# Pooled attention with a gated feed-forward layer on one core: issue order written by hand, images on one queue, first queries and results transposed on TensorE, weights issued after the images, five tiles of lead

## Chip, cores and metric

The kernel runs on one core of one Trainium2 chip. The metric is device time in microseconds (us) of one execution; the kernel before has a median of 1116.38 us over three runs (1113.78 to 1118.0). TensorE (PE), VectorE (DVE), ScalarE (ACT), GpSimd (POOL) and SyncE (SP) each execute their own instruction list in order; SP, ACT and POOL also start DMAs.

## What is computed

```python
# q: 4 x 12288 x 128, kv: 4 x 384 x 32 x 128, all float32
kv_pool = kv.reshape(B, H//4, 4, W//4, 4, C).mean(axis=(2, 4))   # 4x4 means: 768 keys per image
k = v = kv_pool.reshape(B, 768, C) @ w_sr
a = softmax(q @ k.T / sqrt(C));   x = a @ v                      # 4 x 12288 x 128
out = (maximum(x @ w_gate, 0) * (x @ w_val)) @ w_out             # 128 -> 1536 -> 128
```

## The kernel before

The 4 x 12288 queries are cut into 96 tiles of 512 (24 per image b). The 768 pooled keys of an image are six chunks (`jc`) of 128; the 1536 hidden columns are twelve blocks (`fb`) of 128. For a tile k the stages are:

- `scores(k, jc)`: one 128x512 matmul (line 153) and the exponential on ACT (line 154) into `aT`.
- `values(k, jc, half)`: small matmuls (line 165) that add up over jc; after the last, DVE casts the sums to `x16` (line 172) and takes reciprocals of the row sums (line 173). A DMA transpose on SP's queue (line 177) then turns `x16` into `xT`, which the feed-forward stage reads. The softmax division is applied once, squared, at the very end (`inv2`), since the output is quadratic in x.
- `value_proj`, `gate_proj` and `out_proj(k, fb)`: matmuls of lines 185, 196 and 210. ACT copies the value block to `val` (line 189), DVE forms `hT = max(gate, 0) * val` (line 199), and after twelve blocks DVE scales the result into `o_sb` (line 217), which SP stores (line 220).

One pass of the main loop ("loop k", k from 3 to 98) has twelve steps. At each step it issues a piece of `out_proj(k-4)`, `value_proj(k-3)`, `scores(k)` or `values(k-1)` in turn, and `gate_proj(k-3)`. So the feed-forward stage runs `LAG = 3` tiles behind the scores. Ahead of the loop a prelude computes the keys of image 0 chunk by chunk: four DMAs of 256 KB bring a chunk as four lines (`kv_load`, line 103), DVE adds the lines (`pool_lines`, lines 112 and 114), PE transposes and adds the columns (line 128), ACT copies (line 133), PE projects with `w_sr` (lines 135 and 136, float32), ACT scales into `kv16` (line 140), and then come the scores of tiles 0 to 3, and the values of tiles 0 and 1 one chunk behind. The images 1 to 3 are pooled by POOL inside the loop, and `project` stands at step 7 of six loops of each image.

Queries come in groups of four tiles (2048 rows): `q_load` casts float32 to float16 on POOL's software queue (line 75), `q_turn` transposes the group with a DMA transpose on SP's queue (line 85). The feed-forward weights are three casting DMAs on POOL's queue (lines 256 to 258).

The program is written in this sequence, but the framework's scheduler reorders the instructions of each engine by its own estimates, subject to data dependencies. It moves the weights' DMAs to the start, puts half of image 0's loads on ACT's queue, and brings the loads of image 1 forward as buffers (three `kv_in` slots) come free. Eight semaphore lanes (`DMAHW0` to `DMAHW7`) serve the DMAs of SP and ACT: a DMA waits until the one issued eight before it has landed. All PSUM tiles share eight banks.

Of the kernel before, what the change touches and what calls it, by code (L numbers as in the profile page):

```python
# [16 lines left out]
def kernel(  # L17
# [18 lines left out]


    nc = tc.nc

# [13 lines left out]
    NG = NT // GRP  # L53
    LAG = 3
    qk_scale = 1.0 / math.sqrt(C)
# [11 lines left out]

    q16s, qTs = {}, {}

# [10 lines left out]
    def q_turn(g):  # L80
# [5 lines left out]
        qTs[g] = qT  # L86

    def qT_of(k):
        s0 = (k % GRP) * NS
        return qTs[k // GRP][:, s0 : s0 + NS, :].rearrange("c s p -> c (s p)")  # L90
# [6 lines left out]
    def kv_load(b, jc, engines):  # L97
        parts = work.tile([128, r, r, C], FP32, tag="kv_in", bufs=3)
        rows = kv[b, jc * HC : (jc + 1) * HC].rearrange(
            "(hp dh) (wp dw) c -> dh hp wp (dw c)", dh=r, dw=r  # L100
        )
        for dh in range(r):
            engines[dh % len(engines)].dma_start(  # L103
                parts[:, dh].rearrange("p dw c -> p (dw c)"), rows[dh]
            )
        kv_in[b, jc] = parts

    def pool_lines(eng, b, jc):
        parts = kv_in.pop((b, jc))
        s2 = work.tile([128, 2, r, C], FP32, tag="kv_s2")  # L110
        for i in range(2):
            eng.tensor_tensor(s2[:, i], parts[:, 2 * i], parts[:, 2 * i + 1], op=ALU.add)  # L112
        s1 = work.tile([128, r, C], FP32, tag="kv_s1")
        eng.tensor_tensor(s1, s2[:, 0], s2[:, 1], op=ALU.add)
        return s1
# [7 lines left out]

    def project(b, jc, pooled, copy_a, copy_b):
        tp = bank([128, 128])
# [6 lines left out]
        kvT = work.tile([128, 128], FP32, tag="kvT")  # L132
        copy_a(kvT, tp)  # L133
        pr = bank([128, 2, 128])
        nc.tensor.matmul(pr[:, 0, :], w_sr_f32, kvT, start=True, stop=True)  # L135
        nc.tensor.matmul(pr[:, 1, :], kvT, w_sr_f32, start=True, stop=True)  # L136
        copy_b(kv16[:, b, jc, 0 : 2 * C], pr.rearrange("p i c -> p (i c)"))

# [16 lines left out]

    def values(k, jc, half):
        if jc == 0:
# [12 lines left out]
        if jc == NJC - 1:  # L170
            own = slice(2 * half, 2 * half + 2)
            nc.vector.tensor_copy(x16s[k][:, own, :], x_ps[:, :, 0:C])  # L172
            nc.vector.reciprocal(rinvs[k][:, own], x_ps[:, :, C])  # L173
            if half == 1:
                x16 = x16s.pop(k)
                xT = work.tile([128, NS, 128], FP16, tag="xT", bufs=6, name="xT")
                nc.sync.dma_start_transpose(xT, x16.rearrange("p s c -> p (s c)"))
                xTs[k] = xT.rearrange("c s p -> c (s p)")
                rinv = rinvs.pop(k)
                inv2s[k] = work.tile([128, NS, 1], FP32, tag="inv2", bufs=6, name="inv2")  # L180
                nc.vector.tensor_tensor(inv2s[k][:, :, 0], rinv, rinv, op=ALU.mult)

# [22 lines left out]
    def out_proj(k, fb):  # L205
# [8 lines left out]
        if fb == NFB - 1:  # L214
            hTs.pop(k)
            o_sb = work.tile([128, NS, 128], FP32, tag="o_sb", bufs=3)
            nc.vector.tensor_tensor(  # L217
                o_sb, o_banks.pop(k), inv2s.pop(k).to_broadcast([128, NS, 128]), op=ALU.mult
            )
            nc.sync.dma_start(  # L220
# [3 lines left out]
            )  # L224


    w_sr_f32 = const.tile([128, C], FP32)
    nc.sync.dma_start(w_sr_f32, w_sr)
    q_load(0)
    hw = [nc.sync, nc.scalar]  # L230
    kv_load(0, 0, hw)
    kv_load(0, 1, hw)
    ident = const.tile([128, 128], FP32)
    make_identity(nc, ident)
    nc.gpsimd.memset(kv16[:, :, :, 2 * C : 2 * C + 4], 1.0)
    q_turn(0)
    q_load(1)

# [3 lines left out]

    LEAD = GRP
    for jc in range(NJC):
        if jc + 2 < NJC:
            kv_load(0, jc + 2, hw)
        s1 = pool_lines(nc.vector, 0, jc)
        project(0, jc, s1, nc.scalar.copy, act_scaled)
        for k in range(LEAD):
            scores(k, jc)  # L250
# [4 lines left out]
        if jc == 2:  # L255
            nc.gpsimd.dma_start(wv16, moe_w_val)
            nc.gpsimd.dma_start(wg16, moe_w_gate)
            nc.gpsimd.dma_start(wo16, moe_w_out.rearrange("(fb f) c -> f fb c", f=128))
    for k in range(2):
        for half in range(2):  # L260
            values(k, NJC - 1, half)
    q_turn(1)
    q_load(2)


    last = NT + LAG - 1
    kv_s3 = {}
    for k in range(LAG, last + 1):
        g, ph = divmod(k, GRP)
        if ph == 0 and k > LAG:  # L270
            q_turn(g + 1)
            q_load(g + 2)
        b = k // NST + 1
        at = k % NST - (NST - NJC - 6)
        for step in range(NFB):
# [5 lines left out]
            if step % 2 == 0:  # L281
                if LEAD <= k < NT:
                    scores(k, step // 2)
            elif 2 <= k - 1 < NT:
                half, i = divmod(step // 2, NJC // 2)
# [4 lines left out]
            if b < B:  # L290
# [40 lines left out]
```

## Time and profile before

| | before |
|---|---|
| median of 3 runs | 1116.38 us (1113.78 to 1118.0) |
| profiled execution, own time | 1116.32 us |
| its span, first to last instruction | 1114.4 us |
| PE busy | 1041.0 us (93%) |
| DVE busy | 918.9 us (82%) |
| ACT busy | 904.8 us (81%) |
| POOL busy | 104.3 us (9%) |
| mean granted TensorE clock | 0.989 of full |

A row of a timeline reads: start in us, length in us, engine and line, operation, written tile <- read tiles, shape, count merged into the row (x4), and in brackets the idle time of that engine just before, with what ended it. "SPq" and "ACTq" rows are the DMA instructions of those engines. In a windows row the columns are the stretch, its length, busy time and number of instructions of PE, PE's weight loads, DVE, ACT and POOL, the granted clock, the DMA engines' busy share and GB/s. A DMA queue's row gives packets, MB that were written, and the time of its packets as a share of 16 engines; q1 is SP's queue, q10 ACT's, q0 POOL's software queue.

### The profile page before, as it was taken

The page shows a single profiled execution, that of the slowest core. Times are in us where ns is not written, and L with a number is a line of the kernel's source. Part 1 is how long each engine was busy: PE and PEld are TensorE (multiplying, and loading weights), DVE is VectorE, ACT ScalarE, POOL GpSimd, SP SyncE. Part 2 cuts the span into 40 slices and gives each one's busy share as a digit, 9 for nine tenths or more (in the row PEclk, how much of TensorE's full clock was granted, in tenths as well). Part 3 has the DMA queues.
Part 4 walks back from the last instruction along what each step waited for, and adds up shares of the span by engine and source line. Part 5 has one row for each costly group of instructions (what it writes and reads, how often), then busy time and mean ns, then how long its engine had stood idle before and what let it go on. Part 6 is the DMA issues. An engine that isn't in the chain of part 4 may idle for free.

```text
span 1114.4 us, 26042 instructions
## 1 busy us (share of the span) xinstructions
PE 1041.0 (93%) x9930; PEld 688.4 (62%) x9930; DVE 918.9 (82%) x1782; ACT 904.8 (81%) x1741; POOL 104.3 (9%) x124
## 2 busy tenths in 40 slices
PE   0538999999999999999999999999999999999998
PEld 0315666666666666666666666666666666666665
DVE  1328788888888888888888888888798898888888
ACT  0527888878888888878888888888788888888886
POOL 1183000044200000033100000000000000000000
PEclk9969999999999999999999999999999999999999
DMA  9999324256543133132231331341332331211111
GB/s 236 240 226 242 61 49 81 63 124 141 121 81 67 44 77 72 44 68 62 49 82 38 74 81 34 78 76 35 67 72 54 67 63 41 51 44 36 38 44 44
DMA packets 135357, 91.01 MB, mean 82 GB/s; under 512 B 107200, under 2 KB 107328, under 8 KB 135232
## 3 DMA queue, kind: packets, MB, share of 16 engines
q1 hardware_dynamic: 128208, 72.44, 28.1%
q0 software_dynamic: 5296, 13.76, 7.1%
q10 hardware_dynamic: 1728, 3.15, 0.9%
q8 instruction: 77, 1.26, 0.5%
q14 instruction: 48, 0.39, 0.1%
HBM read 52.76 MB, written 25.17 MB: 70 GB/s over the span
## 4 chain that ended last, share of the span: by engine, by line
PE 87%; DMA 6%; SPq 2%; ACT 2%; DVE 2%; issue 0%; POOL 0%; POOLq 0%; DVEq 0%
PE bank_ps L185 22%; PE bank_ps L196 22%; PE bank_ps L210 21%; PE bank_ps L165 11%; PE bank_ps L153 10%; DMA parts<-in_kv_dram 2%; DMA xT<-x 2%; SPq L85 2%; ACT val L189 2%; DMA qT<-q 2%; DVE hT L199 1%; PE bank_ps L135 1%; ACT aT L154 0%; SPq L103 0%; PE bank_ps L136 0%
## 5 line engine op out<-in xcount | busy, mean ns | idle before, releaser
L199 DVE SCALAR_TENSOR_TENSOR hT<-bank_ps,val 128x512 f16<-128x512 f32 x1152 | 772.3, 687 | 132.4 <-ACT val L189 93.1
L189 ACT CAST val<-bank_ps 128x512 f16<-128x512 f32 x1152 | 676.7, 592 | 162.3 <-PE bank_ps L185 160.8
L210 PEld LDWEIGHTS <-hT 128*128 128x128 f16 x4608 | 349.3, 97 | 200.8 <-issue 6.7
L185 PE MATMUL bank_ps<-xT,wv 128*128 128x512 f16 x1152 | 437.6, 380 | 25.7 <-DMA xT<-x 25.7
L210 PE MATMUL bank_ps<-wo,hT 128*128 128x128 f16 x4608 | 440.4, 219 | 0.9 <-DVE hT L199 0.8
L196 PE MATMUL bank_ps<-xT,wg 128*128 128x512 f16 x1152 | 436.4, 379 | 0.0
L154 ACT ACTIVATE aT<-bank_ps 128x512 f16<-128x512 f32 x576 | 346.8, 606 | 3.1 <-PE bank_ps L153 3.1
L165 PE MATMUL bank_ps<-kv,aT 128*128 128x129 f16 x2304 | 224.3, 220 | 0.1
L153 PE MATMUL bank_ps<-qT,kv 128*128 128x512 f16 x576 | 216.3, 381 | 2.9 <-ACT kv L140 2.9
L165 PEld LDWEIGHTS <-aT 128*128 128x128 f16 x2304 | 177.1, 98 | 66.9 <-issue 1.1
L196 PEld LDWEIGHTS <-wg 128*128 128x128 f16 x1152 | 111.6, 97 | 86.7 <-issue 18.8
L185 PEld LDWEIGHTS <-wv 128*128 128x128 f16 x1152 | 112.9, 98 | 13.0 <-DMA xT<-x 7.7
L172 DVE CAST x<-bank_ps 128x256 f16<-128x256 f32 x192 | 79.7, 415 | 9.8 <-PE bank_ps L165 9.8
L75 POOL DMA_DIRECT2D q<-in_q_dram x24 | 13.2, 549 | 675.0 <-DMA qT<-q 674.2
L217 DVE TENSOR_TENSOR o_sb<-bank_ps,inv 128x512 f32<-128x512 f32 x96 | 65.4, 681 | 0.5 <-PE bank_ps L210 0.5
L153 PEld LDWEIGHTS <-kv 128*128 128x128 f16 x576 | 56.0, 98 | 8.2 <-ACT kv L140 4.1
L112 POOL TENSOR_TENSOR s<-parts 128x512 f32<-128x512 f32 x36 | 45.1, 1267 | 10.5 <-DMA parts<-in_kv_dram 9.6
L135 PE MATMUL bank_ps<-kvT,w_sr_f 128*128 128x128 f32 x48 | 12.0, 333 | 25.9 <-ACT kvT L133 22.2
L112 DVE TENSOR_TENSOR s<-parts 128x512 f32<-128x512 f32 x12 | 8.3, 692 | 30.6 <-DMA parts<-in_kv_dram 30.6
L173 DVE RECIPROCAL rinv<-bank_ps 128x2 f32<-128x2 f32 x192 | 30.8, 160 | 0.0
L133 ACT ACT_TABLE_LOAD x1 | 1.3, 1283 | 33.2 <-DMA parts<-in_kv_dram 33.2
L135 PEld LDWEIGHTS bank_ps<-kvT,w_sr_f 128*128 128x128 f32 x48 | 7.3, 193 | 30.5 <-ACT kvT L133 23.7
(23 smaller groups left out, 117.8 us busy)
## 6 DMA issues: line engine op xcount, KB each, us to landing
out_dram<-o_sb SPq DMA_DIRECT2D x96, 256.0 KB, 2.2
parts<-in_kv_dram SPq DMA_DIRECT2D x84, 256.0 KB, 6.5
q<-in_q_dram POOLq DMA_DIRECT2D x24, 512.0 KB, 5.2
parts<-in_kv_dram ACTq DMA_DIRECT2D x12, 256.0 KB, 8.7
xT<-x SPq DMA_TRANSPOSE x96, 2.5
wv<-in_moe_w_val_dram POOLq DMA_DIRECT2D x1, 384.0 KB, 12.1
wg<-in_moe_w_gate_dram POOLq DMA_DIRECT2D x1, 384.0 KB, 14.8
wo<-in_moe_w_out_dram POOLq DMA_DIRECT2D x1, 384.0 KB, 23.9
```

The lines of the kernel that those rows point to most:

```text
L112: eng.tensor_tensor(s2[:, i], parts[:, 2 * i], parts[:, 2 * i + 1], op=ALU.add)
L153: nc.tensor.matmul(s_ps, kv16[:, k // NST, jc, 0:C], qT_of(k), start=True, stop=True)
L154: nc.scalar.activation(aTs[k][:, jc, :], s_ps, AF.Exp, scale=qk_scale)
L165: nc.tensor.matmul(x_ps[:, i, :], aTs[k][:, jc, s * 128 : (s + 1) * 128], kv16[:, k // NST, jc, C : 2 * C + 1], start=(jc == 0 and i == 0) ...
L172: nc.vector.tensor_copy(x16s[k][:, own, :], x_ps[:, :, 0:C])
L173: nc.vector.reciprocal(rinvs[k][:, own], x_ps[:, :, C])
L185: nc.tensor.matmul(va_ps, wv16[:, fb * 128 : (fb + 1) * 128], xTs[k], start=True, stop=True)
L189: nc.scalar.copy(val, va_ps)
L196: nc.tensor.matmul(g_ps, wg16[:, fb * 128 : (fb + 1) * 128], xTs[k], start=True, stop=True)
L199: nc.vector.scalar_tensor_tensor(hTs[k][:, fb, :], g_ps, 0.0, vals.pop((k, fb)), op0=ALU.max, op1=ALU.mult)
L210: nc.tensor.matmul(o_ps[:, s, :], hTs[k][:, fb, s * 128 : (s + 1) * 128], wo16[:, fb, :], start=(fb == 0 and s == 0), stop=(fb == NFB - 1) ...
L217: nc.vector.tensor_tensor(o_sb, o_banks.pop(k), inv2s.pop(k).to_broadcast([128, NS, 128]), op=ALU.mult)
```

## The change

The framework's scheduler is switched off (`manual_schedule`): every engine gets its instructions in the order in which the program issues them. The program is rewritten to suit.

- **Start.** ACT loads its table with a dummy exponential; POOL builds `ident` and a float16 copy, `ident16`. All loads of the prelude go on SP's queue in the order of use: `w_sr`, the first quarter of the first queries in float32, chunk 0, the other three quarters, chunks 1 to 5. `kv_in` has six slots instead of three.
- **First queries.** Group 0 is no longer cast by POOL and turned by DMA; PE transposes each quarter (16 float32 transposes in all) and DVE copies it to float16 (`q_turn_pe`).
- **POOL.** It adds two of the line pairs (chunks 3 and 4). Only behind these does it issue the second query group, and the weights, `w_val` and `w_gate` in halves.
- **Prelude's end.** `project` is split into `turn_pooled` and `project`, with values of the chunk before in between. The prelude now also does the values of tiles 2 and 3 and the scores of tile 4. The results of tiles 0 and 1 are turned by PE (`x_turn_pe`: 8 float16 transposes, two DVE copies); from tile 2 on by the DMA as before.
- **Loop.** `LEAD = LAG = 5`: loop k (from 5 to 100) holds `out_proj(k-6)`, `value_proj(k-5)` and `gate_proj(k-5)`. So five loops at the end have no scores, where there were three. In the loop `turn_pooled` is at step 7 and `project` at step 9. The query turns are one loop later in their group. From output 91 on ACT scales `o_sb` in four pieces.

```diff
-    LAG = 3
+    LEAD = GRP + 1
+    LAG = LEAD
...
-        parts = work.tile([128, r, r, C], FP32, tag="kv_in", bufs=3)
+        parts = work.tile([128, r, r, C], FP32, tag="kv_in", bufs=6)
...
+    def q_turn_pe(i):
+        q32 = q32s.pop(i)
+        qt_ps = bank([128, NS, 128])
+        for s in range(NS):
+            nc.tensor.matmul(
+                qt_ps[:, s, :], q32[:, s, :], ident, is_transpose=True, start=True, stop=True
+            )
...
+        nc.vector.tensor_copy(qTs[0][:, i * NS : (i + 1) * NS, :], qt_ps)
...
+    def x_turn_pe(k):
+        x16 = x16s.pop(k)
+        xt_ps = bank([128, NS, 128], FP16)
+        for s in range(NS):
+            nc.tensor.transpose(xt_ps[:, s, :], x16[:, s, :], ident16)
...
+        nc.vector.tensor_copy(xT, xt_ps)
...
+            if k + LAG + 1 > NT:
+                for s in range(NS):
+                    nc.scalar.mul(o_sb[:, s, :], o_ps[:, s, :], inv2[:, s])
...
+    ctx.enter_context(tc.manual_schedule())
...
+    q_load_plain(0)
+    kv_load(0, 0, [nc.sync])
+    for i in range(1, GRP):
+        q_load_plain(i)
+    for jc in range(1, NJC):
+        kv_load(0, jc, [nc.sync])
...
     for jc in range(NJC):
+        s1 = pool_lines(nc.vector, 0, jc, nc.gpsimd if jc in (3, 4) else None)
+        if jc == 3:
+            q_load(1)
+        if jc == 4:
+            for own in (slice(0, D_FF // 2), slice(D_FF // 2, D_FF)):
+                nc.gpsimd.dma_start(wv16[:, own], moe_w_val[:, own])
+                nc.gpsimd.dma_start(wg16[:, own], moe_w_gate[:, own])
+            nc.gpsimd.dma_start(wo16, moe_w_out.rearrange("(fb f) c -> f fb c", f=128))
+        if jc == 0:
+            q_turn_pe(0)
+        kvT = turn_pooled(s1, nc.scalar.copy)
         if jc > 0:
             for k in range(2):
                 for half in range(2):
-                    values(k, jc - 1, half)
...
+                    values(k, jc - 1, half, turn=False)
+        project(0, jc, kvT, act_scaled)
+        for k in range(GRP):
+            if jc == 0 and k > 0:
+                q_turn_pe(k)
+            scores(k, jc)
+    q_turn(1)
+    q_load(2)
     for k in range(2):
         for half in range(2):
-            values(k, NJC - 1, half)
...
+            values(k, NJC - 1, half, turn=False)
+    for jc in range(NJC):
+        values(2, jc, 0)
+    for k in range(2):
+        x_turn_pe(k)
+    for jc in range(NJC):
+        values(2, jc, 1)
+    for jc in range(NJC):
+        scores(GRP, jc)
+        values(3, jc, 0)
+    for jc in range(NJC):
+        values(3, jc, 1)
...
-    for k in range(LAG, last + 1):
+    for k in range(LEAD, last + 1):
         g, ph = divmod(k, GRP)
-        if ph == 0 and k > LAG:
+        if ph == 1:
             q_turn(g + 1)
             q_load(g + 2)
...
                 if step == 7 and 0 <= at - 4 < NJC:
-                    project(b, at - 4, kv_s3.pop((b, at - 4)), nc.vector.tensor_copy, dve_scaled)
+                    kv_Ts[b, at - 4] = turn_pooled(kv_s3.pop((b, at - 4)), nc.vector.tensor_copy)
+                if step == 9 and 0 <= at - 4 < NJC:
+                    project(b, at - 4, kv_Ts.pop((b, at - 4)), dve_scaled)
```

ACT's list at the start, before. `parts` are image lines, `kvT` the transposed chunk, `bank_ps` PSUM; the brackets name the semaphores that an instruction waits for.

```order
L103 DMA parts_178<-in_kv_dram 128x1x512 [waits DMAHW1_49,DMAHW6_49,DMAHW0_49,DVE_49]
L103 DMA parts_178<-in_kv_dram 128x1x512 [waits DMAHW3_49]
L103 DMA parts_222<-in_kv_dram 128x1x512 [waits DMAHW6_49,DMAHW4_49,DVE_49]
L103 DMA parts_222<-in_kv_dram 128x1x512 [waits DMAHW0_49]
L133 ACT_TABLE_LOAD
L133 COPY kvT_107<-bank_ps_102 128x128 [waits PE_49]
L140 ACTIVATE kv16_64<-bank_ps_109 128x256 [waits PE_49]
```

ACT's list at the start, now (line 272 is the dummy exponential, 156 the copy, 166 the scaling, 180 the exponential):

```order
L272 ACT_TABLE_LOAD
L272 ACTIVATE warm_67<-warm_67 128x1 [waits DVE_49]
L156 COPY kvT_138<-bank_ps_133 128x128 [waits PE_49]
L166 ACTIVATE kv16_64<-bank_ps_140 128x256 [waits PE_49]
L180 ACTIVATE aT_144<-bank_ps_145 128x512 [waits PE_49]
```

Twelve image loads that stood ahead of ACT's first copy are gone from its list.

SP's list before, where the first results are turned: `x16_163` and `x16_171` are the results of tiles 0 and 1, `parts_2877` and `parts_3091` lines of image 1.

```order
L103 DMA parts_2877<-in_kv_dram 128x1x512 [waits DMAHW6_49]
L103 DMA parts_2877<-in_kv_dram 128x1x512 [waits DMAHW7_49]
L103 DMA parts_3091<-in_kv_dram 128x1x512 [waits DMAHW0_49,Pool_49]
L103 DMA parts_3091<-in_kv_dram 128x1x512 [waits DMAHW1_49]
L85 DMA_TRANSPOSE qT_1256<-q16_486 128x16x128 [waits DMAHW2_49,DMASW6_49,PE_49]
L177 DMA_TRANSPOSE xT_343<-x16_163 128x4x128 [waits DMAHW3_49,DVE_49]
L177 DMA_TRANSPOSE xT_355<-x16_171 128x4x128 [waits DMAHW4_49,DVE_49]
```

SP's list now, from the last lines of image 0 on (line 124 the image loads, 88 the query turn, 207 the result turn; `q16_263` is query group 1, `x16_398` and `x16_452` are the results of tiles 2 and 3):

```order
L124 DMA parts_113<-in_kv_dram 128x1x512 [waits DMAHW3_49]
L124 DMA parts_113<-in_kv_dram 128x1x512 [waits DMAHW4_49]
L88 DMA_TRANSPOSE qT_373<-q16_263 128x16x128 [waits DMAHW5_49,DMASW0_49]
L207 DMA_TRANSPOSE xT_445<-x16_398 128x4x128 [waits DMAHW6_49,DVE_49]
L207 DMA_TRANSPOSE xT_500<-x16_452 128x4x128 [waits DMAHW7_49,DVE_49]
L88 DMA_TRANSPOSE qT_502<-q16_375 128x16x128 [waits DMAHW0_49,DMASW6_49]
```

The loads of image 1 are no longer ahead of the first results, and the results of tiles 0 and 1 are not on this queue any more. The turn of group 1 stands behind all of image 0, and `scores(4, jc)` in the prelude reads it.

PE's list in mid-loop, before:

```order
L185 LDWEIGHTS wv_90
L185 MATMUL bank_ps<-xT,wv_90 128x512
L153 LDWEIGHTS kv_64
L153 MATMUL bank_ps<-qT,kv_64 128x512
L196 LDWEIGHTS wg_89
L196 MATMUL bank_ps<-xT,wg_89 128x512
L210 LDWEIGHTS hT
L210 MATMUL bank_ps<-wo_91,hT 128x128
```

and now:

```order
L221 LDWEIGHTS wv_119
L221 MATMUL bank_ps<-xT,wv_119 128x512
L179 LDWEIGHTS kv_64
L179 MATMUL bank_ps<-qT,kv_64 128x512
L232 LDWEIGHTS wg_118
L232 MATMUL bank_ps<-xT,wg_118 128x512
L246 LDWEIGHTS hT
L246 MATMUL bank_ps<-wo_120,hT 128x128
```

Nothing moved here: value projection, scores, gate projection and output projection follow one another as before; lines 221, 179, 232 and 246 are the old 185, 153, 196 and 210.

More of the change, by code (lines that the diff above doesn't have):

```diff
@@ L132, in project @@
         kvT = work.tile([128, 128], FP32, tag="kvT")
-        copy_a(kvT, tp)
+        copy(kvT, tp)
+        return kvT
+    def project(b, jc, kvT, copy):
         pr = bank([128, 2, 128])
@@ L154, in scores, with values @@
         nc.scalar.activation(aTs[k][:, jc, :], s_ps, AF.Exp, scale=qk_scale)
-    def values(k, jc, half):
+    def values(k, jc, half, turn=True):
         if jc == 0:
```

75 lines of the change are left out of this document (38 added, 37 removed).

## Prediction

> **What bounds the kernel now.** I read the windows first, cut where the character of the work changes:
>
> ```profile
> 0.00:34.00 34.00, 1.09 (x4) 0.72 (x4) 7.13 (x11) 0.78 (x1) 4.56 (x13) 1.00 1.06 234
> 34.00:61.00 27.00, 18.19 (x116) 11.11 (x117) 8.81 (x18) 16.37 (x37) 8.46 (x9) 0.98 1.10 244
> 61.00:76.80 15.80, 0.00 (x0) 0.00 (x0) 0.00 (x0) 0.00 (x0) 14.31 (x16) 0.50 1.05 231
> 76.80:113.10 36.30, 30.00 (x256) 18.52 (x255) 28.28 (x53) 25.41 (x48) 14.71 (x13) 0.95 1.03 229
> 113.10:1081.20 968.10, 963.54 (x9266) 638.95 (x9267) 846.82 (x1651) 840.60 (x1620) 62.30 (x75) 1.00 0.29 65
> 1081.20:1114.40 33.20, 28.17 (x289) 19.07 (x287) 27.85 (x51) 21.60 (x38) 0.00 (x0) 0.96 0.15 49
> ```
>
> From 113.1 on PE is busy 963.5 of 968.1 us at full clock: the loop is bound by PE and there is nothing to win in it but small waits. Ahead of that PE has worked 49.3 us of 113.1 (1.09 + 18.19 + 30.00), and the DMA engines are full all the time. So the head is the place. ACT's timeline shows its first part:
>
> ```profile
> 13.96 19.24 ACTq L103 DMA_DIRECT2D parts<-in_kv_dram  x6
> 33.22 1.28 ACT L133 ACT_TABLE_LOAD   x1 [33.22 <-DMA parts<-in_kv_dram]
> 34.52 0.27 ACT L133 COPY kvT<-bank_ps 128x128 f32<-128x128 f32 x1
> 39.31 0.27 ACT L133 COPY kvT<-bank_ps 128x128 f32<-128x128 f32 x1
> ...
> 54.84 0.30 ACT L133 COPY kvT<-bank_ps 128x128 f32<-128x128 f32 x1
> 56.80 2.06 ACT L154 ACTIVATE aT<-bank_ps 128x512 f16<-128x512 f32 x4 [0.48 <-PE bank_ps L153]
> ```
>
> ACT's first compute instruction stands behind its image loads, which wait for lanes and buffers, until 33.2. Then six chunks pass with all data there: the first takes 4.79 us from copy to copy, the others (54.84 - 39.31) / 4 = 3.88 us, a round trip between ACT and PE. Next, SP's queue:
>
> ```profile
> 67.65 6.62 SPq L85 DMA_TRANSPOSE qT<-q  x1
> 74.37 2.52 SPq L177 DMA_TRANSPOSE xT<-x  x2
> ```
>
> The results of tiles 0 and 1 are ready at 60.6 (DVE's rows below) and are turned at 74.4, because SP works through image 1 and a query turn first. That is the empty window 61 to 76.8. PE's timeline gives the lengths of loops:
>
> ```profile
> 113.18 0.39 PE L185 MATMUL bank_ps<-xT,wv 128*128 128x512 f16 x1 [3.21 <-DMA xT<-x]
> ...
> 223.60 0.38 PE L185 MATMUL bank_ps<-xT,wv 128*128 128x512 f16 x1
> ...
> 226.56 0.49 PE L135 MATMUL bank_ps<-kvT,w_sr_f 128*128 128x128 f32 x2 [0.20 <-DVE kvT L133]
> ...
> 235.28 0.38 PE L185 MATMUL bank_ps<-xT,wv 128*128 128x512 f16 x1
> ...
> 601.28 0.38 PE L185 MATMUL bank_ps<-xT,wv 128*128 128x512 f16 x1
> ...
> 611.80 0.38 PE L185 MATMUL bank_ps<-xT,wv 128*128 128x512 f16 x1
> ...
> 1081.24 0.39 PE L210 MATMUL bank_ps<-wo,hT 128*128 128x128 f16 x4
> ...
> 1090.46 0.39 PE L210 MATMUL bank_ps<-wo,hT 128*128 128x128 f16 x4
> ```
>
> Twelve steps of a plain loop: 611.80 - 601.28 = 10.52. A loop with a chunk of a later image: 235.28 - 223.60 = 11.68, so 1.16 more. 90 loops (6 to 95) make 946.8, 18 chunks 20.9, together 967.7; the window has 968.1. The first loop without scores takes 9.22 (1081.24 to 1090.46).
>
> **The change, part by part.** I build the span anew: when loop 5 starts, then the loops, then the end.
>
> *Image 0.* Everything of the prelude is on SP's queue now, 64 KB and 28 x 256 KB, 7.4 MB. The queues' rows for 60 to 70 us, the query rows of 70 to 80 and 60 to 70, and below them the queues' rows for 10 to 20 us:
>
> ```profile
> q1 hardware_dynamic: 1278, 2.33, 95.1%
> q0 software_dynamic: 69, 0.22, 10.8%
> ...
> q<-in_q_dram POOLq DMA_DIRECT2D x1, 512.0 KB, 9.9
> ...
> qT<-q SPq DMA_TRANSPOSE x1, 8.7
> ...
> q0 software_dynamic: 616, 0.99, 53.3%
> q10 hardware_dynamic: 620, 1.14, 32.6%
> q1 hardware_dynamic: 618, 0.67, 23.9%
> ```
>
> SP's queue fills the engines alone: 2.33 + 0.22 MB in 10 us, 255 GB/s. POOL's queue writes 0.22 MB in 1.08 us of engine time, 204 GB/s. When both have work, POOL's gets half (53.3 against 32.6 + 23.9). With 2 us allowed for the start, chunk 0 (1.38 MB with what stands ahead) is there at 7.4, chunk 3 (5.31 MB) at 22.8, and chunk 5 at 31 if nothing disturbs. But behind chunk 3 and one POOL add,
>
> ```profile
> L112 POOL TENSOR_TENSOR s<-parts 128x512 f32<-128x512 f32 x36 | 45.1, 1267 | 10.5 <-DMA parts<-in_kv_dram 9.6
> ```
>
> at 24.1, POOL starts query group 1 and then the weights. The last 2.1 MB of images need until 32.3 at the full rate and until 40.6 at half; I take the middle, 36.4, since POOL's queue has work most but not all of the time.
>
> *The chunks.* PE's and DVE's rows for one chunk, and DVE's for the first results:
>
> ```profile
> 13.71 1.09 PE L128 MATMUL bank_ps<-ident,s 128*128 128x128 f32 x4 [13.71 <-DVE s L114]
> 34.84 0.79 PE L135 MATMUL bank_ps<-kvT,w_sr_f 128*128 128x128 f32 x2 [20.03 <-ACT kvT L133]
> 39.63 0.49 PE L135 MATMUL bank_ps<-kvT,w_sr_f 128*128 128x128 f32 x2 [0.35 <-ACT kvT L133]
> 40.82 1.04 PE L153 MATMUL bank_ps<-qT,kv 128*128 128x512 f16 x4 [0.48 <-ACT kv L140]
> ...
> 12.88 0.69 DVE L114 TENSOR_TENSOR s<-s 128x512 f32<-128x512 f32 x1
> ...
> 57.78 0.42 DVE L172 CAST x<-bank_ps 128x256 f16<-128x256 f32 x1 [9.85 <-PE bank_ps L165]
> ...
> 60.33 0.29 DVE L181 TENSOR_TENSOR inv<-rinv 128x4 f32<-128x4 f32 x1
> ```
>
> Two adds (1.4) and the turn (1.1) lie between a chunk's landing and ACT's copy. By the data, chunk 5 is copied at 36.4 + 2.5 = 38.9. By the round trips: chunk 0 at 9.9; its 4.79; three query turns in between, which the trace does not show as such: four float32 transposes 1.09 by the row above, a DVE copy 0.69 like the add of that size, a score 0.48, so 3 x 2.26 = 6.8 (nothing if the exponentials hid them); then four chunks of 3.88: 37.0. The data decide, by little. ACT's loads being gone from its list, the 33.2 us wait has no successor there.
>
> *To loop 5.* From copy to last exponential 58.86 - 54.84 = 4.0: 42.9. DVE finished the results of tiles 0 and 1 at 60.62, 1.8 after the last exponential: 44.7. New on that path: a cast for tile 2 (0.5) ahead of the two copies of the turned results (0.69 each at most; the eight float16 transposes lie beside these, between nothing and the 2.2 of float32 ones). PE goes on with half of tile 2, scores(4) and values(3), 42 matmuls, about 3.4 us by the scores' 0.22 and a quarter of 0.22 for small ones. From the second turn, about 45.1, that is 48.5. scores(4) needs group 1: issued 24.1, landed within 9.9, turned within 8.7 more: 42.7, so hidden by some 3 us; the weights have 16 us until then.
>
> *Loops.* Loop 5 has no output projection and is set by ACT: 18 instructions at about 0.5 (four take 2.06 in a row): 9.0. Loops 6 to 95: 946.8. The chunks of later images lose the 0.20 wait for `kvT`, since the projection stands two steps (1.75) later: 18 x 0.96 = 17.3; bounds 0.76 (the wait delayed more than itself) and 1.36 (two PSUM banks are held longer). The stalls for `xT` (3.21 at 113.18) go: a result is now turned three loops ahead.
>
> *End.* ACT's row for the loop without scores and values:
>
> ```profile
> 1091.10 9.76 ACT L189 CAST val<-bank_ps 128x512 f16<-128x512 f32 x15 [0.30 <-PE bank_ps L185]
> ```
>
> A step takes (9.76 - 0.59) / 14 = 0.655, a loop 7.86. There were 33.2 us behind loop 95; two more such loops and 0.2 for ACT's four pieces in place of one DVE instruction: 49.1. DVE has no `o_sb` there, ACT no exponentials, so I add nothing.
>
> *Sum.* 48.5 + 9.0 + 946.8 + 17.3 + 49.1 = 1070.7 us of span. The profiled execution took 1116.32 for a span of 1114.4, so 1.9 more: 1072.6, say **1073 us**, against a median of 1116.38, from which that execution hardly differs.
>
> In a sentence that the sum does without: the Trainium skill (DMA: Bandwidth & Descriptors, section Bandwidth) puts a core's share of the memory at about 358 GB/s; the trace shows 255 with these 2 KB rows, and at the page's rate the round trips (37.0) would decide and the sum be 1.9 lower.
>
> **The rivals.**
>
> *Group 1 comes late.* Its turn competes with the weights. If it takes twice 8.7, it lands at 51.4, scores(4) starts some 6 us later, and the time is 1079. Against: image 0 has landed by then.
>
> *TensorE stays at half clock in the prelude.* The granted clock was 0.50 in the idle window, and the first projection took 0.79 against 0.49 later, the first chunk 4.79 against 3.88. In the prelude PE waits for data between chunks. Five cold chunks cost 5 x 0.91 = 4.6 (41.6 in place of 38.9: 2.7), and a cold loop start 0.05 x 36.3 = 1.8, by the window's 0.95: 1077. For it: much of PE's new work is transposes. The Trainium skill (TensorE: Matmul & The Clock Gate, Parts 1 and 4) has the clock halved after about 3.4 us of idleness, and transposes not counted as work; the rows at 34.84 and 39.63 fit the first, none here shows the second.
>
> *The hand-kept order lets PE wait once in every loop, and it is slower than before.* ACT's instructions add up to more than a loop:
>
> ```profile
> L189 ACT CAST val<-bank_ps 128x512 f16<-128x512 f32 x1152 | 676.7, 592 | 162.3 <-PE bank_ps L185 160.8
> L154 ACT ACTIVATE aT<-bank_ps 128x512 f16<-128x512 f32 x576 | 346.8, 606 | 3.1 <-PE bank_ps L153 3.1
> ```
>
> Twelve copies of 592 ns and six exponentials of 606 make 10.74 us in a loop of 10.52; only because they overlap does ACT keep up. If the new order breaks that at one place, PE waits there 96 times. My gain is 43.7 us; over 90 loops it is eaten at 0.49 us a loop, and the kernel is slower by more than 0.5% (about 5.6 us, what a measurement of this kernel can tell from no change) from 0.55 a loop on: 1122 and above. At 0.2 a loop it would be 1091. Against: in mid-loop PE's list is the same as before, row by row, and DVE and ACT serve it in the same turn.
>
> *It does not do what it says.* The loads fill the engines anyway, and the head stays as long; then the time stays near 1116. Against: before, 26 MB (229 to 244 GB/s for 113 us) went through the head; the prelude needs 7.4 MB of images and queries, 0.5 of group 1 and 1.2 of weights.
>
> **How the numbers follow.** The forecast 1073, with its own range 1064 to 1081 (image 0 between 32.3 and 40.6, though the round trips stop the gain at 1.9; the chunks between 0.76 and 1.36; half of each end), 0.68. Late group 1, 0.12. Half clock, 0.10. An order that costs 0.1 to 0.4 a loop but stays ahead of before (1082 to 1109), 0.05. The same time, 0.03. Slower, 0.02. The range 1062 to 1086 holds the first three and the lower part of the fourth, and the low end leaves room for DMAs that run faster than 255 GB/s together with chunks at 0.76. Faster by over 0.5%: 0.68 + 0.12 + 0.10 + 0.05 = 0.95; same 0.03; slower 0.02.
>
> **What the new profile would show.** Right: ACT's first copy near 10 us instead of 34.5; the last exponential of the prelude's first four tiles near 43; the first value projection near 48.5, and no wait of PE for `xT` behind it; plain loops of 10.52, loops with a chunk near 11.5; 49 us behind loop 95. Wrong: scores(4) waiting for `qT`; a granted clock near 0.5 in the prelude; a plain loop above 10.6; projections whose loops still take 11.7; or image 0 landing outside 32 to 41. A total above 1086 would mean that the loop itself has changed, one below 1062 that the prelude is not held by its loads.

## The result, and the profile after

The changed kernel takes 1075.69 us (median of four runs, 1073.74 to 1076.85) against 1117.19 for the kernel before on the same chip: a ratio of 0.963, 95% interval 0.9602 to 0.9658. The forecast was 1073. The profiled execution took 1073.74 us for a span of 1071.8; the prediction's sum was 1070.7.

The windows of the changed kernel, cut at 34 us and at the start of loop 5, of loop 6 and of loop 96 (the first without scores), with the columns of before:

```profile
0.00:34.00 34.00, 17.20 (x84) 11.46 (x84) 15.32 (x21) 10.04 (x22) 8.82 (x17) 1.00 0.98 250
34.00:55.47 21.47, 13.67 (x115) 8.70 (x116) 4.14 (x19) 10.80 (x23) 0.54 (x1) 0.92 1.21 99
55.47:63.77 8.30, 8.26 (x58) 4.27 (x55) 7.29 (x16) 8.08 (x18) 0.00 (x0) 1.00 0.84 107
63.77:1021.20 957.43, 957.13 (x9272) 639.27 (x9270) 857.92 (x1657) 845.03 (x1623) 100.37 (x110) 1.00 0.37 80
1021.20:1071.80 50.60, 44.02 (x433) 29.07 (x431) 40.79 (x72) 39.32 (x81) 0.00 (x0) 0.96 0.15 43
```

The head is 55.5 us, and behind it PE is busy 957.1 of 957.4 us. DMA traffic has left the second half of the head (99 GB/s from 34 us on), where before it ran at 229 to 244 GB/s until 113. ACT's timeline, to be laid beside the one of before:

```profile
12.29 0.27 ACT L156 COPY kvT<-bank_ps 128x128 f32<-128x128 f32 x1 [10.06 <-PE bank_ps L151]
...
24.14 0.27 ACT L156 COPY kvT<-bank_ps 128x128 f32<-128x128 f32 x1 [1.92 <-PE bank_ps L151]
...
28.98 0.30 ACT L156 COPY kvT<-bank_ps 128x128 f32<-128x128 f32 x1
...
40.65 0.30 ACT L156 COPY kvT<-bank_ps 128x128 f32<-128x128 f32 x1
41.74 0.38 ACT L166 ACTIVATE kv<-bank_ps 128x256 f16<-128x256 f32 x1 [0.80 <-PE bank_ps L162]
42.61 2.06 ACT L180 ACTIVATE aT<-bank_ps 128x512 f16<-128x512 f32 x4 [0.48 <-PE bank_ps L179]
```

The first copy comes at 12.3 us instead of 34.5, the last exponential of the first four tiles ends at 44.7 instead of 58.9. PE's timeline, at the end of the head, in two loops with a chunk, in a plain loop and at the end:

```profile
51.51 0.61 PE L179 MATMUL bank_ps<-qT,kv 128*128 128x512 f16 x1 [5.08 <-DMA qT<-q]
...
220.80 0.27 PE L151 MATMUL bank_ps<-ident,s 128*128 128x128 f32 x1
222.66 0.38 PE L161 MATMUL bank_ps<-kvT,w_sr_f 128*128 128x128 f32 x2
233.73 0.38 PE L161 MATMUL bank_ps<-kvT,w_sr_f 128*128 128x128 f32 x2
...
600.10 0.38 PE L221 MATMUL bank_ps<-xT,wv 128*128 128x512 f16 x1
610.61 0.38 PE L221 MATMUL bank_ps<-xT,wv 128*128 128x512 f16 x1
...
1066.89 0.40 PE L246 MATMUL bank_ps<-wo,hT 128*128 128x128 f16 x4 [1.30 <-DVE hT L235]
```

Three things to see. The scores of tile 4 wait 5.08 us for the turned queries of group 1: that is the rival "Group 1 comes late". A plain loop is 10.51 us, as before; a loop with a chunk 233.73 - 222.66 = 11.07, so a chunk costs 0.56, not the 0.96 of the prediction. And at the very end PE waits 1.30 us for a block.

### The profile page after: what moved, and what is told of

It is laid out like the page before. It is cut to its first block, busy times and chain, and to the rows that moved or that the text cites. A ratio compares the mean times of both kernels' runs of the same rounds, so it can differ in the third digit from the quotient of the medians.

```text
span 1071.8 us, 26152 instructions
## 1 busy us (share of the span) xinstructions
PE 1040.3 (97%) x9954; PEld 692.8 (65%) x9954; DVE 925.5 (86%) x1782; ACT 913.3 (85%) x1762; POOL 109.7 (10%) x128
## 4 chain that ended last, share of the span: by engine, by line
PE 94%; DMA 4%; ACT 0%; SPq 0%; DVE 0%; POOL 0%; issue 0%; ACTq 0%; POOLq 0%; DVEq 0%
PE bank_ps L246 24%; PE bank_ps L232 23%; PE bank_ps L221 23%; PE bank_ps L191 12%; PE bank_ps L179 11%; DMA parts<-in_kv_dram 2%; DMA qT<-q 2%; DMA q<-in_q_dram 1%; PE bank_ps L162 0%; PE bank_ps L161 0%; DVE hT L235 0%; PE bank_ps L151 0%; ACT o_sb L256 0%; POOL s L133 0%; SPq L124 0%
## 5 line engine op out<-in xcount | busy, mean ns | idle before, releaser
L235 DVE SCALAR_TENSOR_TENSOR hT<-bank_ps,val 128x512 f16<-128x512 f32 x1152 | 763.1, 686 | 102.0 <-ACT val L225 68.0
L133 POOL TENSOR_TENSOR s<-parts 128x512 f32<-128x512 f32 x38 | 49.0, 1291 | 180.9 <-DMA parts<-in_kv_dram 119.0
L258 DVE TENSOR_TENSOR o_sb<-bank_ps,inv 128x512 f32<-128x512 f32 x91 | 61.9, 680 | 0.0
L137 POOL TENSOR_TENSOR s<-s 128x512 f32<-128x512 f32 x18 | 22.9, 1270 | 1.4
L203 DVE TENSOR_TENSOR inv<-rinv 128x4 f32<-128x4 f32 x96 | 19.0, 198 | 3.3
L151 PE MATMUL bank_ps<-ident,s 128*128 128x128 f32 x42 | 9.7, 308 | 5.9 <-DVE s L137 5.7
```

The source lines that it names most:

```text
L133: (other if i and other else eng).tensor_tensor(s2[:, i], parts[:, 2 * i], parts[:, 2 * i + 1], op=ALU.add)
L235: nc.vector.scalar_tensor_tensor(hTs[k][:, fb, :], g_ps, 0.0, vals.pop((k, fb)), op0=ALU.max, op1=ALU.mult)
L258: nc.vector.tensor_tensor(o_sb, o_ps, inv2.to_broadcast([128, NS, 128]), op=ALU.mult)
```

## The experiments

Twelve kernels ran. Each was measured beside the kernel before on the same chip, whose medians there were 1115.1 to 1116.1 us, and ratios are to that. A kernel that was measured several times has a ratio with its 95% interval; a single run is named so. The changed kernel was measured in another run (before: 1117.19), so small differences from it are uncertain by some 2 us.

**1. Who brings the gain: the order by hand, or the rewriting?** Two runs, one part alone each. The rewritten program with the scheduler on:

```diff
-    ctx.enter_context(tc.manual_schedule())
```

> The rewritten program, with the framework's scheduler ordering each engine again. Theory G (the order by hand brings the gain, the rewriting alone little): the scheduler pulls the weights to the start and image 1 forward again (six slots), the head is long again, and the time is 1100 to 1117. Rival H (the rewritten program brings it, whoever orders it: no image loads on ACT, first turns on PE, five tiles of lead): within 5 us of the changed kernel, 1071 to 1081.

Measured: 1083.52 us, ratio 0.9711 (0.9685 to 0.9737), 8 more than the changed kernel. And the kernel before with only this line put in ahead of its first DMA:

> The kernel before, word for word, with only the scheduler switched off: image 0 still half on ACT's queue, first queries cast and turned by DMA, the weights behind chunk 2, three tiles of lead. Theory G (the scheduler's order was the fault): image 1 is not in the head any more, the first results are turned as soon as they are there, the empty 15.8 us go and so do most of the 33 us at the start: 1080 to 1095. Rival H: the written order, made for a scheduler, waits in other places, and it stays at 1105 or above.

Measured: 1107.31 us, ratio 0.9922 (0.9892 to 0.9953). Theory G misses in both. Theory H misses the first by 2.5 us and holds in the second: the written order does wait in another place. Under the scheduler the rewritten program is 32 us faster than the kernel before, and the order by hand alone brings 8. The windows of the rewritten program under the scheduler show image 1 in the head again, and at first no harm:

```profile
61.00:77.00 16.00, 15.96 (x137) 9.63 (x136) 15.04 (x29) 15.00 (x31) 13.72 (x15) 1.00 1.03 228
77.00:113.00 36.00, 35.91 (x350) 23.82 (x349) 32.93 (x63) 31.96 (x62) 14.74 (x13) 1.00 1.09 229
```

The loads run at 229 GB/s, and PE is busy 15.96 of 16 us beside them. So full DMA engines alone do not hold PE up; it matters what stands behind the loads in a list. Loop 5 starts at 56.99, only 1.5 us later than in the changed kernel. The harm comes in loop 10, which takes 17.81 us instead of 10.51. Rows of SP and DVE, and the window of that loop:

```profile
96.28 8.99 SPq L124 DMA_DIRECT2D parts<-in_kv_dram  x10
105.94 8.13 SPq L88 DMA_TRANSPOSE qT<-q  x1
...
114.80 2.13 SPq L207 DMA_TRANSPOSE xT<-x  x1
118.68 0.42 DVE L198 CAST x<-bank_ps 128x256 f16<-128x256 f32 x1 [5.26 <-DMA xT<-x]
108.19:126.00 17.81, 13.50 (x106) 8.36 (x104) 9.45 (x19) 9.70 (x19) 0.57 (x1) 0.81 1.00 213
```

The turn of tile 6's result, which DVE had cast by 87.8, stands behind image loads and a query turn and is issued at 114.80. There are three `x16` buffers, so DVE's cast for tile 9 waits for that turn to land, and PE waits 4.31 us for DVE; the loop's mean granted clock is 0.81. Loop 11 takes 11.52. These two loops lose 8.3 us; with the 1.5 of the head, and an end that is 0.7 shorter, that is the difference to the changed kernel (8.9 us of span). In the kernel before with the order by hand, the first output is scaled at 76.4 us instead of 95.9, and the second 22.8 us earlier (before, then by hand):

```profile
109.69 0.68 DVE L217 TENSOR_TENSOR o_sb<-bank_ps,inv 128x512 f32<-128x512 f32 x1
...
86.94 0.68 DVE L217 TENSOR_TENSOR o_sb<-bank_ps,inv 128x512 f32<-128x512 f32 x1
```

But its time fell by some 8 only. PE's waits say where the rest went:

```profile
PE bank_ps L135 <- DVE kvT L133: 20.8, 18, 1.2
```

Eighteen waits of 1.2 us for the copied chunk, one in each loop with a chunk of a later image. Under the scheduler these had been 0.20. A loop with a chunk takes 12.49 us here instead of 11.68, and 18 x 0.81 = 14.6 of the 22.8 are lost again; the span is 8.8 us shorter.

**2. The split of the projection.** The changed kernel with the projection back at step 7:

```diff
-                if step == 9 and 0 <= at - 4 < NJC:
+                if step == 7 and 0 <= at - 4 < NJC:
```

> The changed kernel with the projection of a later image's chunk back at step 7, right behind the turn. In the changed kernel a loop with a chunk takes 11.07 us against 10.51 for a plain one (0.55 more, and the timeline shows no wait of PE in it); before it was 1.16 more, of which 0.20 was the wait for the copied chunk. Theory E (the two steps between turn and projection removed all of the 0.6): a loop with a chunk takes 11.6 to 11.7 again, 18 x 0.6 = 11 us, span 1082, ratio about 0.973. Rival F (the split removed only the wait of 0.20, and the rest went because the scheduler no longer places the chunk's instructions): 11.3, 18 x 0.2 = 3.6, span 1075.5, ratio about 0.967.

Measured: 1101.9 us, ratio 0.9877 (0.9847 to 0.9906): 26 us more than the changed kernel, over twice what the larger expectation said. PE's timeline of this kernel in two loops with a chunk:

```profile
217.25 0.49 PE L161 MATMUL bank_ps<-kvT,w_sr_f 128*128 128x128 f32 x2 [1.15 <-DVE kvT L156]
...
229.74 0.49 PE L161 MATMUL bank_ps<-kvT,w_sr_f 128*128 128x128 f32 x2 [1.15 <-DVE kvT L156]
```

and DVE's in front of the second:

```profile
227.08 1.43 DVE L235 SCALAR_TENSOR_TENSOR hT<-bank_ps,val 128x512 f16<-128x512 f32 x2
228.80 0.69 DVE L235 SCALAR_TENSOR_TENSOR hT<-bank_ps,val 128x512 f16<-128x512 f32 x1 [0.29 <-ACT val L225]
229.41 0.28 DVE L156 COPY kvT<-bank_ps 128x128 f32<-128x128 f32 x1
```

The chunk is turned on PE at 228.3 (0.27 us). Its copy stands behind products in DVE's list, the last of which itself waits for ACT, and is done at 229.69; PE, whose next instruction is the projection, stands. A loop with a chunk is 229.74 - 217.25 = 12.49, 1.42 more than 11.07, and 18 x 1.42 = 25.6 us. In the changed kernel the copy runs from 221.89 to 222.17 and the projection comes at 222.66: two steps hide it with 0.5 us to spare.

So the order by hand takes away the placing that the scheduler had done, and the split gives it back with some more. In the rewritten program under the scheduler, which has the split too, a loop with a chunk also takes 11.07 (rows of line 161 at 210.37 and 221.44): the split form costs 0.56 under either order. The test of both edits together is the kernel before with these two edits alone:

```diff
+    ctx.enter_context(tc.manual_schedule())
...
                 if step == 7 and 0 <= at - 4 < NJC:
-                    project(b, at - 4, kv_s3.pop((b, at - 4)), nc.vector.tensor_copy, dve_scaled)
+                    kv_Ts[b, at - 4] = turn_pooled(kv_s3.pop((b, at - 4)), nc.vector.tensor_copy)
+                if step == 9 and 0 <= at - 4 < NJC:
+                    project(b, at - 4, kv_Ts.pop((b, at - 4)), dve_scaled)
```

> The kernel before with two edits only: the scheduler switched off, and the projection of a later image's chunk two steps behind its turn. With the scheduler off alone the kernel before took 1107.3 us, and TensorE waited 1.15 us for the copied chunk in each of 18 loops. Theory J (order by hand and split belong together and make most of the gain): the 18 waits and the rest of the joined form go, 18 x 1.42 = 25.6, so 1081.7 us; what is left to the changed kernel, 6 us, is the prelude. Rival K (in the old program with three tiles of lead the split wins less, since the loop has other waits): 1090 or above.

Measured: 1081.43 us, ratio 0.969 (0.9669 to 0.9711), 0.3 from the expectation. Its loops with a chunk:

```profile
213.20 0.38 PE L138 MATMUL bank_ps<-kvT,w_sr_f 128*128 128x128 f32 x2
...
224.27 0.38 PE L138 MATMUL bank_ps<-kvT,w_sr_f 128*128 128x128 f32 x2
```

11.07 again, and no wait for `kvT` is left in them. Two small edits make some 34 of the 41 us: by the second output 22.5 are won in the head, and 18 x 0.61 = 11.0 in the loops. On top of them one queue for the images, the first queries and results on TensorE, the late weights and five tiles of lead, all together, make the other 6. These shares hold for this order of adding alone, since the rewriting with the split, under the scheduler, makes 32 by itself. The old program with the split alone, under the scheduler, was not run, and the 6 us are not divided further except by experiments 5 and 6.

**3. What holds the turn of group 1?** SP issues it at 32.45; in the issue rows of the changed kernel it lands 19.0 us later, where the 22 later ones take 4.3 us at the least and 4.6 in the median. The queues' rows for 30 to 40 us, then 40 to 50, then 50 to 60:

```profile
q0 software_dynamic: 2165, 1.55, 116.6%
q1 hardware_dynamic: 381, 0.10, 17.6%
...
q1 hardware_dynamic: 1035, 0.26, 95.8%
q0 software_dynamic: 178, 0.38, 37.9%
...
q1 hardware_dynamic: 2256, 0.55, 41.9%
q0 software_dynamic: 144, 0.52, 31.6%
```

First POOL's queue (q0) has the engines, and from 32.45 to 36.5 us no packet of the turn moves at all. Then, from 40 to 50 us, the turn's packets (q1) take 16 x 10 us x 0.958 / 1035 = 148 ns each. W_out lands at 48.0 and query group 2 at 50.3, and in the next 1.3 us, 50.3 to 51.6, q1 is alone:

```profile
q1 hardware_dynamic: 1011, 0.24, 93.4%
```

That is 16 x 1.3 x 0.934 / 1011 = 19 ns a packet. (The whole of 50 to 60 us gives 30 ns, but packets of result turns and of the next query turn are among these; some of a result turn's are in the narrow window too.) Two transfers stand beside the turn, so I held back each alone, then both, behind the last values of tiles 0 and 1 (a POOL copy of one column of tile 0's result stands ahead of the DMA):

```diff
-            nc.gpsimd.dma_start(wo16, moe_w_out.rearrange("(fb f) c -> f fb c", f=128))
...
     q_turn(1)
-    q_load(2)
...
+    hold = const.tile([128, 1], FP16)
+    nc.gpsimd.tensor_copy(hold, x16s[0][:, 0, 0:1])
+    nc.gpsimd.dma_start(wo16, moe_w_out.rearrange("(fb f) c -> f fb c", f=128))
+    q_load(2)
```

> w_out alone is issued behind the last values of tiles 0 and 1 on POOL; query group 2 stays at 31.5. In the changed kernel the turn of group 1 was issued at 32.45, took SP 10.93 us and landed 19.0 us later, at 51.5, and loop 5 started at 55.5. Theory A (the POOL queue's transfers hold the turn's 256-byte packets back, 148 ns each from 40 to 50 us against 30 ns later): the turn lands earlier, since one of the two transfers that stand in its way is gone; if it is w_out's 1536 short rows that count, at 45 or before, loop 5 at about 50.4 and the span some 5 us less (1067); if it is the queries, no change. Rival B (the turn of a whole group is slow by itself while image 0 and the weights have just come): it lands at 51.5 again, loop 5 at 55.5, span 1071.8.

> Query group 2 alone is issued behind the last values of tiles 0 and 1 on POOL; w_out stays at 30.5. Theory A: the turn of group 1 has only w_out beside it. If the queries' transfer is what slows it, it lands at 45 or before, loop 5 starts at about 50.4, span 1067; if w_out, it lands at 50 to 51.5 and nothing moves. Rival B: 51.5 and 55.5 again, span 1071.8.

> Both w_out and query group 2 are issued behind the last values of tiles 0 and 1 on POOL. Theory A: the turn of group 1 lands 5 to 9 us after its issue, as the 22 later turns do (4.3 to 4.6 us), so at 38 to 42; SP's 10.93 us for it shrink to about 2; the PE's wait of 5.08 us for it is gone, loop 5 starts at about 50.4 and the span is 1066 to 1067 (time 1068 to 1071, ratio to before about 0.957). Rival B (the turn is slow by itself): 51.5, 55.5, 1071.8 again. What could come in its place: w_out and group 2 land at 52 to 54, and are not asked for before loop 6 and loop 8.

The issue row of the turn in the changed kernel, with w_out late, with group 2 late, and with both late:

```profile
qT<-q SPq DMA_TRANSPOSE x1, 19.0
```

```profile
qT<-q SPq DMA_TRANSPOSE x1, 9.9
```

```profile
qT<-q SPq DMA_TRANSPOSE x1, 10.1
```

```profile
qT<-q SPq DMA_TRANSPOSE x1, 7.0
```

Times: 1069.41 (one run), 1068.18 (one run) and 1068.82 (ratio 0.9577, 0.9559 to 0.9594). Rival B is out. But I had expected one of the two to be the culprit, and either one's absence is enough: the turn lands at 41 to 42, before PE asks at 46, and the wait of 5.08 us is gone in all three. With both late loop 5 starts here:

```profile
48.62 0.38 PE L221 MATMUL bank_ps<-xT,wv 128*128 128x512 f16 x1
```

That is 6.9 us sooner, more than the wait. Another 1.3 is the clock: in the changed kernel the matmuls behind the wait take 0.61 us instead of 0.38 (row at 51.51) and follow one another every 0.43 us instead of 0.22, and from the first score of tile 4 to loop 5 it takes 3.96 us instead of 2.66. The last 0.5 is in the chain ahead, which came that much sooner in this run. The medians differ by 6.9 as well (by the ratios, 5.9). The Trainium skill (TensorE: Matmul & The Clock Gate, Part 1) has TensorE at half rate after about 3.4 us of idleness; the trace agrees, 0.61 to 0.63 behind a wait of 5.08. The Trainium skill also says (DMA: Bandwidth & Descriptors, section Queues, rings and completion order) that a DMA engine takes packets from its queues in turn; the trace agrees where both queues have packets to move: they moved 91 packets each from 37.5 to 39 us. The 381 against 2165 of 30 to 40 us come mostly from the time before 36.5, in which the turn moved nothing. Why a packet of the turn takes up to 148 ns meanwhile, the runs do not show.

**4. Data or round trips?** In the prelude of the changed kernel the copy of a turned chunk moves from ACT to DVE, and DVE's adds go ahead of it:

```diff
-        kvT = turn_pooled(s1, nc.scalar.copy)
+        kvT = turn_pooled(s1s.pop(jc), nc.vector.tensor_copy)
+        for ahead in {1: [2, 3], 2: [4], 3: [5]}.get(jc, []):
+            pooled(ahead)
```

> In the prelude the turned chunk is copied by DVE in place of ACT, with the adds of DVE one to two chunks ahead. In the changed kernel the chunks came every 3.89 us (2.06 of exponentials, 0.30 copy, 0.38 scaling and two waits of 0.80 and 0.48, all on ACT in turn), with the last image data in at 30.6 and the last exponential's end at 44.7. Theory C (the round trips between ACT and PE set the pace, not the data): the copy and the projection go under the exponentials, chunks come every 2.9 us or so, the last exponentials end at 39 to 41; but the scores of tile 4 still wait for the turn of group 1 at 51.5, so loop 5 still starts at 55.5 and the span stays within 0.5 of 1071.8. Rival D (the data set the pace, as the prediction had it): the last exponentials end at 44 or later.

Measured: 1074.75 us (one run). ACT's scaling of two chunks, and PE's scores of tile 4:

```profile
35.97 0.38 ACT L166 ACTIVATE kv<-bank_ps 128x256 f16<-128x256 f32 x1 [0.37 <-PE bank_ps L162]
...
39.27 0.38 ACT L166 ACTIVATE kv<-bank_ps 128x256 f16<-128x256 f32 x1 [0.37 <-PE bank_ps L162]
```

```profile
49.14 0.61 PE L179 MATMUL bank_ps<-qT,kv 128*128 128x512 f16 x1 [5.18 <-DMA qT<-q]
```

Chunks come every 3.30 us, not the hoped 2.9, and the last exponential ends at 42.2, not at 39 to 41; but that is 2.5 earlier with the same data, so the round trips set the pace. The time stays the same (span 1072.9 against 1071.8, one execution each), because tile 4 waits for its queries as before.

**5. Images on two queues.** The changed kernel with half of each load of image 0 on ACT's queue, as before (the expectation speaks of every image; the edit is image 0 alone):

```diff
-    kv_load(0, 0, [nc.sync])
+    kv_load(0, 0, [nc.sync, nc.scalar])
...
-        kv_load(0, jc, [nc.sync])
+        kv_load(0, jc, [nc.sync, nc.scalar])
```

> The changed kernel with the lines of every image loaded half by SP's queue and half by ACT's, as before. Theory L (with six slots and an order by hand the second queue costs nothing or little, the 33 us of the kernel before came from the scheduler's order and the three slots): ACT's twelve loads stand ahead of its first copy, its first copy comes at 13 to 16 us instead of 12.3; the loop is unchanged or, where ACT issues loads of later images, up to 0.1 us longer in 18 loops: span 1070 to 1076. Rival M (ACT's list is blocked by the loads until their lanes are free): ACT's first copy at 25 or later, span 1080 or above.

Measured: 1078.76 us (one run), a span of 1076.8, between the two. ACT's timeline:

```profile
2.24 19.78 ACTq L124 DMA_DIRECT2D parts<-in_kv_dram  x10
22.06 0.27 ACT L156 COPY kvT<-bank_ps 128x128 f32<-128x128 f32 x1 [19.83 <-DMA parts<-in_kv_dram]
```

ACT is blocked by its loads until 22.1, with six slots and no buffer to wait for. That is 9.8 us later than in the changed kernel, of which 3 reach loop 5 (58.5 against 55.5): the rest fell on the wait for group 1, which is not there any more.

**6. Results turned by DMA.** With w_out and group 2 late, the results of tiles 0 and 1 are turned by DMA again (`x_turn_pe` taken out):

> As the kernel with w_out and query group 2 held back, but the results of tiles 0 and 1 turned by DMA on SP's queue as before, not by TensorE. There loop 5 starts at 48.6 and the results of tile 1 were cast at about 45.2. By rows of the changed kernel a DMA turn of a result takes SP 1.2 to 1.9 us and lands 2.5 to 4 us after its issue: the first would land at 47 to 48.5, the second at 49 to 50.5. Theory (TensorE's turn is worth little where the chain ends): loop 5 starts 0 to 1.5 us later, span 1067 to 1068.5. Rival (the queue holds them up as it did before): 3 us later or more.

Measured: 1070.73 us (one run) against 1068.82 with TensorE's turn. Loop 5 starts at 47.5, even 1.1 sooner, with no wait of PE for `xT`. But it lasts 1.5 longer, and loop 6 is 0.4 later. DVE shows why:

```profile
54.53 0.42 DVE L198 CAST x<-bank_ps 128x256 f16<-128x256 f32 x1 [1.97 <-DMA xT<-x]
```

The turn of tile 1's result is issued at 45.21, when w_out and group 2 start, and lands at 54.43; DVE's cast for tile 4 waits for it, and PE waits 1.47 for DVE. The remaining 1.3 us of the span are spread over the later loops (seven waits of the gate projection for `hT`, 2.9 us in all, where the other kernel has 1.1). So TensorE's turn buys 0.4 us up to loop 6; with one run, the total of 1.9 is hardly more than what runs of one kernel differ by (1068.48 to 1070.11).

**7. Together.** Both edits of 3, that of 4, and each query turn of chunk 0 issued one score ahead; then, on top, the last two outputs scaled by DVE:

```diff
-            if jc == 0 and k > 0:
-                q_turn_pe(k)
+            if jc == 0 and k + 1 < GRP:
+                q_turn_pe(k + 1)
...
-            if k + LAG + 1 > NT:
+            if NT - LAG <= k < NT - 2:
```

> Three edits on the changed kernel: w_out and query group 2 held back; the chunk's copy on DVE with the adds ahead; in chunk 0 each query turn issued one score ahead. Measured so far: held back, the turn of group 1 lands at 41 and loop 5 starts at 48.6; the copy on DVE ends the prelude's chain 2.5 us earlier, which gained nothing while the turn landed at 49. If the waits are as these runs showed, the query turns save 3 x 0.8 to 3 x 1.0 more, scores of tile 4 start at 41 to 42 and loop 5 at 43.5 to 44.5: span 1062 to 1063, time 1064 to 1066. Rival: image 0's data (last lines at 30.6) or TensorE at half rate take the place of the round trips, loop 5 at 46 or later, span 1064.5 or above.

> As the kernel with the three edits of the prelude, and besides the last two outputs are scaled by DVE in one instruction and not by ACT in four pieces. In the changed kernel TensorE waited 0.68 and 1.30 us at the end for a block that ACT had put behind such pieces, and the last four pieces took 1.14 us against 0.68 for DVE's one. Theory: 1.0 to 1.8 us less than the same kernel without this edit; rival: DVE, which has twelve products of 0.62 in such a loop, is late itself, and it gains 0.5 or less.

Measured: 1064.61 (ratio 0.9536, 0.9516 to 0.9555) and 1063.12 us (0.9528, 0.951 to 0.9545). Loop 5 starts at 45.0 (0.5 later than expected at most) and 43.8. The last wait of PE and DVE's last scaling in the second:

```profile
1056.80 0.40 PE L246 MATMUL bank_ps<-wo,hT 128*128 128x128 f16 x4 [0.80 <-DVE hT L235]
```

```profile
1057.23 0.69 DVE L258 TENSOR_TENSOR o_sb<-bank_ps,inv 128x512 f32<-128x512 f32 x1 [0.49 <-PE bank_ps L246]
```

The wait falls from 1.30 to 0.80, and 0.69 stand for 1.14. From ACT's last run of four casts (1045.93 and 1045.22) to the end of the span the two kernels take 16.94 and 16.01 us, so the edit is worth 0.9, just below the expectation; the two intervals overlap. The rest of the difference is not the edit's: loop 5 starts 1.2 us sooner in the second kernel, whose prelude is the same. The last kernel is some 12 us faster than the changed one.

## Why the prediction was right, and where it was not

The total held (1073 against 1075.69), in part because errors cancel: the head ended 7.0 us later than forecast, loop 5 took 0.7 less, the 90 loops 6.7 less, the end 1.5 more.

- *Image 0* was wrong. I took the last data at 36.4 within 32.3 to 40.6; DVE adds the last lines at 30.63. From 10 to 20 us SP's queue alone moved 2.83 MB, 283 GB/s, where I had read 255:

```profile
q1 hardware_dynamic: 1552, 2.83, 105.6%
```

  And POOL's queue, with group 1 from 24.6 and the weights from 28.4 on, came too late to take half.
- *The chunks*: "The data decide, by little" fell (experiment 4). The other branch did hold: three query turns in 6.7 us (14.96 to 21.62) against 6.8, and 3.89 per chunk against 3.88. The chain started 2.4 us later than I had it (copy at 12.29 against 9.9), and chunk 1 was still at half rate, 4.84 (24.14 to 28.98): copy of chunk 5 at 40.65, forecast 38.9.
- *To loop 5*: "landed 42.7, so hidden by some 3 us" is the step that failed. It came at 51.5: the turn took 19.0 us and not 8.7, which was the row of a turn that had only image loads beside it. The profile of before had the warning, in the answer for 10 to 20 us from which I took the queues' rows: there the turn of group 0, issued beside POOL's loads, has the row

```profile
qT<-q SPq DMA_TRANSPOSE x1, 20.3
```

  The rival had the mechanism, its moment (51.4) and its price (6 us; 6.9 measured by experiment 3), and I gave it 0.12, with the argument that image 0 has landed by then. That was true and beside the point: w_out and group 2 on POOL's queue were in the way, not the image. With the turn in time loop 5 starts at 48.6, the forecast being 48.5, and that is partly luck: the last exponential ends at 44.4 there against 42.9, and what follows takes 4.3 instead of 5.6.
- *Half clock* came true in part: PE's rows are at half rate up to 27 us, which cost about 1.0 in chunk 1 (4.84 against 3.89), and again behind the wait, 1.3 of the 6.9 above.
- *Loops*: 10.51 against 10.52 is right. A chunk was mis-sized: "lose the 0.20 wait" gave 0.96, and 0.56 was measured (18 x 0.4 = 7.2, the 6.7 above). I took everything but the wait for work; the joined form under the order by hand costs 1.98, of which 1.15 are wait. The remainder of 0.83 stands against 0.56 when nothing waits; its projection takes 0.49 where the split one takes 0.38, and what else is in it stays open.
- *A wait once in every loop*: I looked for it in the plain loop, where PE's list had not changed, and it did not come. It was ready in the loops with a chunk, and the split, which I had credited with 3.6 us, keeps 25.6 us out. Right answer, wrong reason: I did not ask what the order by hand would have made of the joined projection.
- *End*: 7.86 a loop is right; "I add nothing" was wrong by 1.5. ACT's four pieces stand ahead of a cast that the last products wait for; with the last two outputs on DVE 0.9 comes back (experiment 7), and the rest is not tested.

## What to carry to other kernels

When a scheduler is switched off, go through every place where one engine waits for another's answer and ask what stands ahead of that answer in the other's list; a distance of two steps was worth 26 us here, under the order by hand. A transfer that fits by the durations of a quiet profile must be checked against what the other queues carry at that moment, and two transfers together can cost far more than either. An engine can be fully served for many loops and still be stopped later, when the backlog in a queue has used up the buffers behind it; so read the loops one by one, not only the head. Where a transfer is late, shortening another chain ahead of the same instruction shows nothing until the transfer is moved.

## What the runs showed of the hardware that I had not expected

- The turn of a query group (a DMA transpose) lands in 7.0 us with neither transfer beside it, in 9.9 and 10.1 with one, in 19.0 with both. The later kernels repeat it: 5.8 to 7.3 with neither (three kernels), 18.7 with both (the kernel of experiment 4). SP itself is held in that instruction for 4.87, 5.98, 5.07 and 10.93 us in the first four.
- The granted-clock column does not show every slow stretch: it reads 1.00 for the first 34 us, though the same four transposes take 1.11 us at 11.1 and 0.66 at 27.7.

```profile
11.14 1.11 PE L151 MATMUL bank_ps<-ident,s 128*128 128x128 f32 x4 [4.27 <-DVE s L137]
...
27.70 0.66 PE L151 MATMUL bank_ps<-ident,s 128*128 128x128 f32 x4
```
